# The inducing points' softmax in one pass over x with running maxima, on four column groups, with weights loaded later and layer 2 six chunks behind layer 1

## The chip, the cores and the metric

The kernel runs on one core of one Trainium2 chip. The metric is device time in microseconds of one execution; less is better. Three executions of the kernel before took 1043.28, 1042.4 and 1047.28 us, median 1043.28 us.

## The reference

`x` has 12480 tokens of 128 channels, `inducing` 32 points of 128 channels, and there are four weights of 128 by 2048 (or its transpose), handed over as float64.

```
h = softmax(inducing @ x.T / sqrt(128)) @ x          # 32 x 128
a = softmax(x @ h.T / sqrt(128)) @ h                 # 12480 x 128
g = a @ moe_w_in;   y1 = max(0.01 * g, g) @ moe_w_out
g = y1 @ moe2_w_in; g = where(g >= 1, g, where(g <= -1, 0, (g + 1)**2 / 4))
out = g @ moe2_w_out
```

## The kernel before

There are two phases. The **prologue** makes `HT`, that is h transposed (`HT` is written at L390). The **main phase** takes x again, transposed, in 26 chunks of 480 tokens, and each chunk through 16 slices of the hidden dimension: 416 steps `k` of layer 1, and 416 of layer 2, which follow `LAG` chunks and six steps later.

The order on every engine is the order in which the program is written (a manual schedule), so each engine works its own list strictly from the top; SyncE's list holds the DMAs.

**Prologue.** x comes in 13 pieces of 960 tokens (`load_x`), and 7 of the 26 chunks come a second time by channel (`xd`); after pieces 2, 4, 6 and 8 a quarter of a weight is loaded. `split_x(c)` transposes a chunk's four blocks on TensorE (L233), copies them out (`xT`, L235), and makes a high part (`xhi`) and a low part (`xlo`, mostly on GpSimd, L242) of the tokens for float32r products. `scores(c)` (L248) is one float32 product of 480 columns against a weight with the 32 points at one of four places and zeros beside them (`izf`), so that four chunks add up to a band of 128 rows. Two groups of bands have a maximum each (`maximum`), so the exponentials (`exps`, L283) start only when the maxima of a group are known; then `turn` (L293, L297, L298) transposes e back in two parts, and `gather` (L310, L311) multiplies it with `xhi` and `xlo`. `factors` and `denominator` bring the two groups together. Everything from the last scores to `HT` comes after x has landed.

**Weights.** `convert(n, q)` makes float32 of a quarter (512 columns) of a float64 weight: one operation on ScalarE (L103), four on VectorE (L104, L106, L108, L110), and then, for the first weight (n = 0), a sum on VectorE (L114), for the others a copy on ScalarE (L117) and two operations on GpSimd (L118, L119). There are 16 quarters (`units`). `work(n)` lists n of VectorE's operations, two quarters in turn; `ensure(n, j)` lists as many as slice j needs. In the program before, the prologue holds the conversions of 8 quarters (`CONV_1`, `WORK_1`, `WORK_2`): all of the first two weights.

**Start of the main phase.** `attend(0, ...)` makes chunk 0's softmax weights `aT`; `hidden(q, ...)` makes quarter q of `Gs` = h w_in (L419, L423, L426), from the first weight; step k multiplies `aT` with slice k of `Gs` (L549), takes `hi` (ScalarE, L552) and `lo` (VectorE, L559, or GpSimd, L557), and four steps later come three products with the second weight (L513 to L515). `linear` (steps 4 to 18) needs the second weight. After 16 slices a chunk of layer 1 ends with `x2hi` (ScalarE, L601) and `x2lo`. Layer 2 has six products of 480 columns a step, `cl`, `sq`, `g`, `hi`, `lo` on the other engines, and ends a chunk with `y` (L611). The conversions of the last 8 quarters stand one operation in every second step.

Of the kernel before, what the change touches and what calls it, by code (L numbers as in the profile page):

```python
# [9 lines left out]
F32 = mybir.dt.float32  # L10
# [60 lines left out]
def moe_kernel(ctx: ExitStack, tc, x_d, xt_d, it_d, w1_d, w2_d, w3_d, w4_d, y_d):  # L71
    """a = softmax(x h^T) with h from the inducing points; y = L4(act2(L3(L2(act1(L1(a h))))))
    with every operand of a large product as a sum of two float32r parts."""
# [5 lines left out]
    raw = ctx.enter_context(tc.tile_pool(name="raw", bufs=RAW))  # L79
    cv = ctx.enter_context(tc.tile_pool(name="cv", bufs=3))  # L80
# [5 lines left out]
    ahead = False       # whether a conversion's end makes place for the next load  # L86
# [42 lines left out]
    def work(n, until=len(units)):  # L129
        """n more operations of the conversions, two quarters in turn, up to a given number of them."""  # L130
# [33 lines left out]
    xe = inner.enter_context(tc.tile_pool(name="xe", bufs=1))  # L164
    xq = inner.enter_context(tc.tile_pool(name="xq", bufs=3))
    iz = inner.enter_context(tc.tile_pool(name="iz", bufs=1))

    xraw, xlo, xT = {}, {}, {}

    def load_x(i):  # L170
        for c in (2 * i, 2 * i + 1):
            if c in XT_DMA:
                t = xq.tile([C, CW], F32, name="xd", bufs=XD)
                nc.sync.dma_start(out=t, in_=xt_d[:, c * CW:(c + 1) * CW])
                xT[c] = t
# [42 lines left out]
    tb = (bank[6], bank[7])

    def rows(s):  # L220
        return min(SC, NCH - s * SC) * M

    def split_x(c):
        """A chunk by channel, and by token in two parts."""
        sl = slice(c * CB, (c + 1) * CB)
        i, h = divmod(c, 2)
        src = xraw[i][:, h * CB:(h + 1) * CB, :]
        if not h:       # the low part takes the place of the piece before
            xlo[i] = xs.tile([BT, 2 * CB, C], F32R, name="xlo", tag=f"x{i - 1}")
        if c not in XT_DMA:  # L230
            b = tb[c // 2 % 2]
            for q in range(CB):
                nc.tensor.transpose(b[:, q * BT:(q + 1) * BT], src[:, q, :], ident[:BT, :BT])  # L233
            t = xq.tile([C, CW], F32, name="xT")
            nc.scalar.activation(t, b[:, :CW], AF.Copy)  # L235
            xT[c] = t
        if c % XHI_DVE == XHI_DVE - 1:
            nc.vector.tensor_copy(out=xhi[:, sl, :], in_=src)
        else:
            nc.scalar.activation(xhi[:, sl, :], src, AF.Copy)  # L240
# [416 lines left out]
```

## Time and profile before

| | us |
|---|---|
| median of three executions | 1043.28 |
| span of the profiled execution (first to last instruction) | 1040.2 |
| median less span | 3.1 |
| `HT` ready | 78.0 |
| first chunk of layer 1 done (`x2hi` starts) | 105.8 |
| fourth chunk of layer 1 done | 154.5 |
| a chunk where both layers run | 36.3 |
| a chunk of layer 2 alone, at the end | 20.9 |

The profile's page is of one execution of 1040.2 us. It gives no time for what lies around the span; the median of the executions is 3.1 us above it. A row of the timeline gives the start, the length, the engine, the line and the tiles, and in brackets how long the engine had been idle and what ended that. A length for "x4" runs from the first start to the last end.

### The profile page before, as it was taken

Reading aid. Unit: us, or ns where it says so; the run is one execution under the profiler, and the core shown is the slowest. Engines: PE = TensorE matmul, PEld = TensorE weight load, DVE = VectorE, ACT = ScalarE, POOL = GpSimd, SP = SyncE. Lnnn points to the kernel's source line nnn. Section 1 sums busy time; section 2 is a strip of 40 time slices with the busy share of each in tenths; the row PEclk is TensorE's granted clock in tenths of the full one; section 3 lists DMA queues with packets and bytes.
Section 4 is the critical chain, followed back from the end, with each engine's and each line's share of the span. In section 5 each row is a group of like instructions: output and inputs, shape, how many; then the busy total and the mean of one; then the engine's idle time right before and its main releaser. Section 6 shows DMA issues by size and latency. Waiting matters only on the chain.

```text
span 1040.2 us, 15657 instructions
## 1 busy us (share of the span) xinstructions
PE 1018.7 (98%) x4956; PEld 862.0 (83%) x4956; DVE 835.2 (80%) x1491; ACT 835.1 (80%) x1605; POOL 686.0 (66%) x561
## 2 busy tenths in 40 slices
PE   8789999999999999999999999999999999999998
PEld 5377878888888888888888888888888888888887
DVE  4987998777787877778787777878877787878998
ACT  4537788888888888888888888888888888888997
POOL 5741647666666666666676666666666666667886
PEclk9989999999999999999999999999999999999999
DMA  9830300000000000000000000000000000000000
GB/s 242 242 92 10 109 12 10 20 1 20 20 1 20 20 20 1 20 20 1 20 20 20 1 20 19 6 15 20 20 1 20 20 10 1 10 10 10 11 10 20
DMA packets 12782, 30.30 MB, mean 29 GB/s; under 512 B 1539, under 2 KB 9091, under 8 KB 12699
## 3 DMA queue, kind: packets, MB, share of 16 engines
q1 hardware_dynamic: 12699, 29.30, 9.7%
q8 instruction: 39, 0.64, 0.3%
q14 instruction: 44, 0.36, 0.1%
HBM read 22.90 MB, written 6.39 MB: 28 GB/s over the span
## 4 chain that ended last, share of the span: by engine, by line
PE 89%; DVE 8%; DMA 2%; ACT 1%; issue 1%; SPq 0%; ACTq 0%; DVEq 0%
PE bank L513 25%; PE bank L515 25%; PE bank L514 25%; PE bank L549 8%; PE bank L471 2%; DVE lo L559 2%; DMA wraw<-in_w 1%; DVE cvb L110 1%; DVE cva L106 1%; DVE cvb L108 1%; PE bank L501 0%; DVE w L114 0%; PE bank L310 0%; PE bank L598 0%; DMA xraw<-in_x 0%
## 5 line engine op out<-in xcount | busy, mean ns | idle before, releaser
L575 POOL TENSOR_TENSOR lo<-g,hi 128x480 fp32r<-128x480 f32 x409 | 499.8, 1225 | 242.4 <-PE bank L514 162.1
L552 ACT ACTIVATE hi<-bank 128x480 fp32r<-128x480 f32 x416 | 236.1, 573 | 132.2 <-PE bank L549 129.7
L515 PE MATMUL bank<-lo,whi 128*128 128x480 f32 x832 | 316.4, 380 | 0.0
L513 PE MATMUL bank<-hi,whi 128*128 128x480 f32 x832 | 316.4, 380 | 0.0
L514 PE MATMUL bank<-hi,wlo 128*128 128x480 f32 x832 | 315.7, 379 | 0.0
L586 DVE SCALAR_TENSOR_TENSOR g<-bank,sq 128x480 f32<-128x480 f32 x416 | 270.0, 649 | 38.9 <-ACT sq L563 38.9
L563 ACT ACTIVATE sq<-cl,half 128x480 f32<-128x480 f32 x416 | 289.2, 695 | 9.6 <-DVE cl L582 5.2
L559 DVE SCALAR_TENSOR_TENSOR lo<-bank,hi 128x480 fp32r<-128x480 f32 x316 | 205.5, 654 | 110.5 <-ACT hi L552 110.2
L582 DVE TENSOR_SCALAR cl<-bank 128x480 f32<-128x480 f32 x416 | 270.4, 650 | 19.7 <-PE bank L515 13.7
L570 ACT ACTIVATE hi<-g 128x480 fp32r<-128x480 f32 x416 | 249.1, 599 | 0.5 <-DVE g L586 0.5
L515 PEld LDWEIGHTS bank<-lo,whi 128*128 128x128 f32 x832 | 156.0, 188 | 26.7 <-POOL lo L557 0.9
L514 PEld LDWEIGHTS bank<-hi,wlo 128*128 128x128 f32 x832 | 156.7, 188 | 25.0
L513 PEld LDWEIGHTS bank<-hi,whi 128*128 128x128 f32 x832 | 156.3, 188 | 24.8 <-ACT y L611 0.4
L557 POOL TENSOR_TENSOR lo<-r,hi 128x480 fp32r<-128x480 f32 x100 | 125.3, 1253 | 60.9 <-ACT r L556 57.5
L549 PE MATMUL bank<-aT,Gs 96*128 96x480 f32 x416 | 162.8, 393 | 0.0
L513 PE MATMUL bank<-x2hi,whi 128*128 128x480 f32 x416 | 159.1, 383 | 0.6 <-DVE g L586 0.6
L515 PE MATMUL bank<-x2lo,whi 128*128 128x480 f32 x416 | 157.9, 380 | 0.0
L514 PE MATMUL bank<-x2hi,wlo 128*128 128x480 f32 x416 | 157.8, 379 | 0.0
L514 PEld LDWEIGHTS bank<-x2hi,wlo 128*128 128x128 f32 x416 | 78.9, 190 | 12.6
L513 PEld LDWEIGHTS bank<-x2hi,whi 128*128 128x128 f32 x416 | 78.8, 190 | 12.6 <-DVE g L586 1.3
L515 PEld LDWEIGHTS bank<-x2lo,whi 128*128 128x128 f32 x416 | 78.1, 188 | 12.7
L549 PEld LDWEIGHTS bank<-aT,Gs 96*128 96x128 f32 x416 | 78.2, 188 | 12.1 <-DVE lo L559 0.4
(115 smaller groups left out, 666.6 us busy)
## 6 DMA issues: line engine op xcount, KB each, us to landing
wraw<-in_w SPq DMA_DIRECT2D x16, 512.0 KB, 4.7
xraw<-in_x SPq DMA_DIRECT2D x13, 480.0 KB, 13.2
xt<-in_xt SPq DMA_DIRECT2D x26, 240.0 KB, 2.7
out_y<-y SPq DMA_DIRECT2D x26, 240.0 KB, 2.0
xd<-in_xt SPq DMA_DIRECT2D x7, 240.0 KB, 13.3
iT<-in_it SPq DMA_DIRECT2D x1, 16.0 KB, 1.9
```

Source lines behind the costliest of these rows:

```text
L513: nc.tensor.matmul(out, lhsT=whi[n][:, sl], rhs=hi, start=start, stop=False)
L514: nc.tensor.matmul(out, lhsT=wlo[n][:, sl], rhs=hi, start=False, stop=False)
L515: nc.tensor.matmul(out, lhsT=whi[n][:, sl], rhs=lo, start=False, stop=stop)
L549: nc.tensor.matmul(p1, lhsT=Gs[:, j * 128:(j + 1) * 128], rhs=aT[c], start=True, stop=True)
L552: nc.scalar.activation(hi, p1, AF.Relu)
L557: nc.gpsimd.tensor_tensor(out=lo, in0=r, in1=hi.bitcast(F32), op=ALU.subtract)
L559: nc.vector.scalar_tensor_tensor(out=lo, in0=p1, scalar=0.0, in1=hi.bitcast(F32), op0=ALU.max, op1=ALU.subtract)
L563: nc.scalar.activation(sq, cls.pop(kb - 1), AF.Square, scale=-0.5, bias=half)
L570: nc.scalar.activation(hi, g, AF.Copy)
L575: nc.gpsimd.tensor_tensor(out=lo, in0=g, in1=hi.bitcast(F32), op=ALU.subtract)
L582: nc.vector.tensor_scalar(out=cl, in0=p3, scalar1=1.0, scalar2=-1.0, op0=ALU.min, op1=ALU.max)
L586: nc.vector.scalar_tensor_tensor(out=g, in0=b3[(kb - 1) % 3][:, :CW], scalar=-1.0, in1=sqs.pop(kb - 1), op0=ALU.max, op1=ALU.add)
```

## The change

- x comes by token in ten bands: the 12480 tokens are four groups of 3120, and a band is `BANDS[s]` tokens of each group. The last two bands come a second time by channel (`xl`), the other `xd` loads are gone, and so are `xhi` and `xlo`.
- `scores(s)` is four float32 products, one for each group, with a weight of 32 columns, into four places of 32 rows of one bank. Each band has its own maximum, the least bias so far (`nm`), its exponentials at once, and a factor `alpha`. `gather(s)` is four float32 products of 32 weight columns for each block of 128 tokens, likewise into four places; `add_up` keeps the running sums `R` and `D`. It follows one band behind.
- Two quarters of weights are loaded between the bands, four more behind x. Two quarters are converted in the prologue (`UNTIL_S`) in place of eight; the first weight's sum goes to GpSimd; `units` is reordered.
- `hidden(2)` and `hidden(3)` stand after steps 1 and 3, with the conversions that they need.
- `LAG` is 6 in place of 4; `warm` is gone.

```diff
-RAW = 4
-LAG = 4
+RAW = 6
+LAG = 6
+G4 = 4
+BANDS = (48, 128, 256, 512, 512, 512, 512, 384, 128, 128)
+XL = 2
+XT_DVE = 4
+LOAD_W = (3, 4)
+WORK_S = ((0, 0), (0, 0), (0, 0), (0, 0), (1, 2), (2, 3), (2, 3), (2, 2), (0, 1), (0, 0))
+UNTIL_S = (0, 0, 0, 0, 1, 2, 2, 2, 2, 2)
+HIDDEN = (1, 3)
...
-            yield
-            nc.vector.tensor_tensor(out=w1[:, sl], in0=a, in1=b, op=ALU.add)
+            nc.gpsimd.tensor_tensor(out=w1[:, sl], in0=a, in1=b, op=ALU.add)
...
-    units = [(n, q) for n in range(4) for q in range(NQ)]
+    units = [(0, 0), (0, 1), (0, 2), (1, 0), (0, 3), (1, 1), (1, 2), (1, 3)] + [(n, q) for n in (2, 3) for q in range(NQ)]
...
+    for s, w in enumerate(BANDS):
+        p, nb = min(w, 128), -(-w // 128)
+        if s == NS_B - XL:
+            xl = xs.tile([C, XL, G4, 128], F32, name="xl")
+            nc.sync.dma_start(out=xl.rearrange("p s q t -> p (s q t)"), in_=xl_d)
...
+        nc.sync.dma_start(out=t.rearrange("p q b c -> p (q b c)"), in_=src)
+        xb[s] = t
+        if s in LOAD_W:
+            load_next_w()
+    load_xt(0)
+    for _ in range(RAW - len(LOAD_W)):
+        load_next_w()
...
+    def by_channel(s):
...
+        for g in range(0, len(flat), 4):
...
+            for i, (q, b) in enumerate(part):
+                nc.tensor.transpose(ps_t[:, i * p:(i + 1) * p], xb[s][:, q, b, :], ident[:p, :p])
+            dst, src = t[:, g * p:(g + len(part)) * p], ps_t[:, :len(part) * p]
+            if k % XT_DVE == 1:
+                nc.vector.tensor_copy(out=dst, in_=src)
+            else:
+                nc.scalar.activation(dst, src, AF.Copy)
+    def scores(s):
+        p = b_S[s % 2]
+        for q in range(G4):
+            nc.tensor.matmul(p[q * M:(q + 1) * M, :w], lhsT=iT, rhs=xT[s][:, q * w:(q + 1) * w], start=True, stop=True)
+        nc.vector.tensor_reduce(out=mx[:, s:s + 1], in_=p[:, :w], op=ALU.max, axis=AX.X)
...
+            nc.vector.scalar_tensor_tensor(out=nm[:, s:s + 1], in0=mx[:, s:s + 1], scalar=-SCALE, in1=nm[:, s - 1:s],
+                                           op0=ALU.mult, op1=ALU.min)
+        nc.scalar.activation(e[:, :w], p[:, :w], AF.Exp, scale=SCALE, bias=nm[:, s:s + 1], accum_out=ssum[:, s:s + 1])
+        if s:
+            nc.scalar.activation(alpha[:, s:s + 1], nm[:, s - 1:s], AF.Exp, scale=-1.0, bias=nm[:, s:s + 1])
+    def turn(s):
+        for b in range(nb):
+            nc.tensor.transpose(b_U[:p, b * 128:(b + 1) * 128], es[s][:, b * p:(b + 1) * p], ident)
+        nc.scalar.activation(t[:p, :nb * 128], b_U[:p, :nb * 128], AF.Copy)
+    def gather(s):
+        for b in range(nb):
+            for q in range(G4):
+                nc.tensor.matmul(A[q * M:(q + 1) * M], lhsT=eTs[s][:p, b * 128 + q * M:b * 128 + (q + 1) * M],
+                                 rhs=xb[s][:, q, b, :], start=(b == 0), stop=(b == nb - 1))
...
+    for s in range(NS_B):
+        if s not in xT:
+            by_channel(s)
+        if s:
+            turn(s - 1)
+        scores(s)
+        work(WORK_S[s][0], UNTIL_S[s])
+        if s:
+            gather(s - 1)
+            add_up(s - 1)
+        work(WORK_S[s][1], UNTIL_S[s])
...
+        if k in HIDDEN:
+            q = 2 + HIDDEN.index(k)
+            ensure(0, 4 * q)
+            for p in range(3):
+                hidden(q, p)
```

**What moved, on TensorE, in the prologue.** Before, around chunks 1 to 4 (four transposes of x, then one product of 480 columns into a bank of 128 rows):

```order
L233 MATMUL bank_85<-ident,xraw 128x120 x4
L248 MATMUL bank_78<-xT,izf 128x480
L233 MATMUL bank_85<-ident,xraw 128x120 x4
L248 MATMUL bank_78<-xd,izf 128x480
L233 MATMUL bank_84<-ident,xraw 128x120 x4
L248 MATMUL bank_78<-xT,izf 128x480 x2
```

and in the change, around one band of 512 (`e` is the band before's exponentials, `eT` those turned):

```order
L227 MATMUL bank_83<-ident,xb 128x128 x4
L227 MATMUL bank_81<-ident,xb 128x128 x4
L227 MATMUL bank_82<-ident,xb 128x128 x4
L227 MATMUL bank_83<-ident,xb 128x128 x4
L257 MATMUL bank_86<-ident,e 128x128 x4
L239 MATMUL bank_84<-xT,iT 32x512 x4
L268 MATMUL bank_87<-xb,eT 32x128 x16
```

The products with e, which stood in one block behind all scores, stand between the bands, and both kinds write 32 rows at a time.

**On VectorE, at the start of the main phase.** Before (`s` is the last of `attend(0)`, `Gs` are `hidden`, the `lo` are steps 0, 1, 2 and so on):

```order
L495 TENSOR_TENSOR s<-ea,s 120x4x32
L426 SCALAR_TENSOR_TENSOR Gs<-bank_80,Gs 32x512
L426 SCALAR_TENSOR_TENSOR Gs<-bank_79,Gs 32x512
L426 SCALAR_TENSOR_TENSOR Gs<-bank_85,Gs 32x512
L559 SCALAR_TENSOR_TENSOR lo_893<-bank_81,hi_892 128x480
L426 SCALAR_TENSOR_TENSOR Gs<-bank_80,Gs 32x512
L559 SCALAR_TENSOR_TENSOR lo_900<-bank_82,hi_899 128x480
L559 SCALAR_TENSOR_TENSOR lo_905<-bank_83,hi_904 128x480
L559 SCALAR_TENSOR_TENSOR lo_910<-bank_84,hi_909 128x480
```

and in the change, from step 0's `lo`:

```order
L484 SCALAR_TENSOR_TENSOR lo_666<-bank_84,hi_665 128x480
L484 SCALAR_TENSOR_TENSOR lo_671<-bank_85,hi_670 128x480
L100 TENSOR_SCALAR cvb<-wraw 128x512 x2
L102 SCALAR_TENSOR_TENSOR cva<-cva,cvb 128x512 x2
L104 TENSOR_SCALAR cvb<-cva 128x512 x2
L106 SCALAR_TENSOR_TENSOR cvb<-wraw,cvb 128x512
L351 SCALAR_TENSOR_TENSOR Gs<-bank_82,Gs 32x512
L484 SCALAR_TENSOR_TENSOR lo_695<-bank_86,hi_694 128x480
L484 SCALAR_TENSOR_TENSOR lo_700<-bank_87,hi_699 128x480
L106 SCALAR_TENSOR_TENSOR cvb<-wraw,cvb 128x512
L100 TENSOR_SCALAR cvb<-wraw 128x512 x2
L102 SCALAR_TENSOR_TENSOR cva<-cva,cvb 128x512 x2
```

Fifteen operations of conversions (seven, then eight) now stand between step 1 and step 4, where there were none.

**On TensorE, the same place.** Before:

```order
L471 MATMUL bank_78<-HT,xt 120x32 x4
L419 MATMUL bank_80<-w_88,HT 96x512
L419 MATMUL bank_79<-w_88,HT 96x512
L419 MATMUL bank_85<-w_88,HT 96x512
L501 MATMUL bank_78<-identr,s 96x120 x4
L419 MATMUL bank_80<-w_88,HT 96x512
L549 MATMUL bank_81<-aT,Gs 128x480
```

and in the change:

```order
L396 MATMUL bank_81<-HT,xt 120x32 x4
L344 MATMUL bank_83<-w_91,HT 96x512
L344 MATMUL bank_82<-w_91,HT 96x512
L426 MATMUL bank_81<-identr,s 96x120 x4
L474 MATMUL bank_84<-aT,Gs 128x480
L474 MATMUL bank_85<-aT,Gs 128x480
L344 MATMUL bank_82<-w_91,HT 96x512
L474 MATMUL bank_86<-aT,Gs 128x480
L474 MATMUL bank_87<-aT,Gs 128x480
L344 MATMUL bank_83<-w_91,HT 96x512
L474 MATMUL bank_88<-aT,Gs 128x480
```

The third and fourth `hidden` product stand behind steps 1 and 3, and the steps behind them wait in TensorE's list.

## Rows read from the trace of the kernel before

**Rows 1.** The page: span, busy time by engine, the chain by engine.

```profile
span 1040.2 us, 15657 instructions
PE 1018.7 (98%) x4956; PEld 862.0 (83%) x4956; DVE 835.2 (80%) x1491; ACT 835.1 (80%) x1605; POOL 686.0 (66%) x561
...
PE 89%; DVE 8%; DMA 2%; ACT 1%; issue 1%; SPq 0%; ACTq 0%; DVEq 0%
```

**Rows 2.** Windows by stage: busy PE, PEld, DVE, ACT, POOL; PEclk, DMA share, GB/s.

```profile
20.00:49.00 29.00, 23.24 (x96) 11.68 (x97) 28.29 (x35) 19.62 (x40) 20.88 (x14) 1.00 0.95 253
49.00:78.00 29.00, 22.57 (x243) 20.78 (x241) 24.18 (x43) 9.37 (x23) 15.00 (x10) 0.82 0.33 103
...
106.00:155.00 49.00, 47.94 (x233) 39.45 (x232) 47.36 (x87) 40.27 (x86) 29.17 (x22) 1.00 0.20 64
```

**Rows 3.** Timeline of VectorE at the end of the prologue.

```profile
73.30 1.05 DVE L346 TENSOR_SCALAR ssum<-ssum,f 128x3 f32<-128x3 f32 x2
...
77.72 0.26 DVE L390 TENSOR_TENSOR HT<-bank,rden 128x96 f32<-128x96 f32 x1 [1.00 <-PE bank L388]
```

**Rows 4.** Timeline of ScalarE: ends of chunks, layer 1 (L601) and layer 2 (L611).

```profile
105.83 0.57 ACT L601 ACTIVATE x2hi<-bank 128x480 fp32r<-128x480 f32 x1
...
154.53 0.58 ACT L601 ACTIVATE x2hi<-bank 128x480 fp32r<-128x480 f32 x1
...
222.56 0.57 ACT L601 ACTIVATE x2hi<-bank 128x480 fp32r<-128x480 f32 x1
...
258.82 0.57 ACT L601 ACTIVATE x2hi<-bank 128x480 fp32r<-128x480 f32 x1
...
997.85 0.57 ACT L611 ACTIVATE y<-bank 128x480 f32<-128x480 f32 x1
...
1018.74 0.57 ACT L611 ACTIVATE y<-bank 128x480 f32<-128x480 f32 x1
```

**Rows 5.** Timeline of VectorE: the first two weight quarters land.

```profile
13.13 0.43 DVE L104 TENSOR_SCALAR cvb<-wraw 128x512 uint32<-128x512 uint32 x1 [4.11 <-DMA wraw<-in_w]
...
19.74 0.43 DVE L104 TENSOR_SCALAR cvb<-wraw 128x512 uint32<-128x512 uint32 x1 [3.29 <-DMA wraw<-in_w]
```

**Rows 6.** Timeline of TensorE: transposes and scores, early and at full clock.

```profile
11.88 1.82 PE L248 MATMUL bank<-xd,izf 128*128 128x480 f32 x2
...
24.88 0.63 PE L233 MATMUL bank<-ident,xraw 120*128 120x120 f32 x4 [0.23 <-DMA xraw<-in_x]
25.35 1.78 PE L248 MATMUL bank<-xT,izf 128*128 128x480 f32 x4
...
28.96 0.98 PE L248 MATMUL bank<-xT,izf 128*128 128x480 f32 x2
```

**Rows 7.** Timeline of TensorE: products with e right behind transposes.

```profile
66.84 0.30 PE L310 MATMUL bank<-xhi,eT 120*64 120x128 f32 x1
66.98 0.22 PE L311 MATMUL bank<-xlo,eT 120*64 120x128 f32 x1
67.04 0.23 PE L310 MATMUL bank<-xhi,eT 120*64 120x128 f32 x1
```

**Rows 8.** Timeline of ScalarE: step 0 of the main phase.

```profile
83.95 0.57 ACT L552 ACTIVATE hi<-bank 128x480 fp32r<-128x480 f32 x1 [0.83 <-PE bank L549]
```

**Rows 9.** Timeline of VectorE: conversions alone, and one beside GpSimd.

```profile
65.08 0.68 DVE L110 SCALAR_TENSOR_TENSOR cvb<-wraw,cvb 128x512 f32<-128x512 uint32 x1
65.68 0.41 DVE L108 TENSOR_SCALAR cvb<-cva 128x512 uint32<-128x512 uint32 x1
...
92.71 1.45 DVE L104 TENSOR_SCALAR cvb<-wraw 128x512 uint32<-128x512 uint32 x1
```

**Rows 10.** Groups by line and form: GpSimd's sum of a quarter.

```profile
L119 POOL TENSOR_TENSOR wlo<-cva,cvb 128x512 fp32r<-128x512 f32 x12 | 16.0, 1335 | 3.4 <-DVE cvb L110 2.8
```

**Rows 11.** Windows: TensorE's clock falls after a wait, and rises.

```profile
54.00:55.00 1.00, 0.26 (x2) 0.26 (x3) 0.66 (x2) 0.00 (x0) 0.00 (x0) 0.80 0.00 0
...
61.00:62.00 1.00, 1.00 (x14) 1.00 (x13) 1.00 (x2) 0.24 (x1) 0.32 (x1) 0.79 0.69 184
```

More of the change, by code (lines that the diff above doesn't have):

```diff
@@ L218, in moe_kernel @@
[L218 to L238, printed above, removed]
-        else:
-            nc.scalar.activation(xhi[:, sl, :], src, AF.Copy)
-        eng = nc.vector if c % XLO_DVE == XLO_DVE - 1 else nc.gpsimd
-        eng.tensor_tensor(out=xlo[i][:, h * CB:(h + 1) * CB, :], in0=src, in1=xhi[:, sl, :].bitcast(F32), op=ALU.subtract)
@@ L244, in scores @@
-    def scores(c):
-        s, q = divmod(c, SC)
-        p = score[s][:, :CW]
-        last = q == SC - 1 or c == NCH - 1
-        nc.tensor.matmul(p, lhsT=izf[:, q].rearrange("p r m -> p (r m)"), rhs=xT.pop(c), start=(q == 0), stop=last)
-        if last:
-            r = rows(s)
-            if r < 128:
-                nc.vector.tensor_copy(out=smax[:, s:s + 1], in_=smax[:, s - 1:s])
-            nc.vector.tensor_reduce(out=smax[:r, s:s + 1], in_=p[:r], op=ALU.max, axis=AX.X)
-    nmax = const.tile([128, 2], F32, name="nmax")
@@ L285, in exps @@
         es[s] = e
     def turn(s):
-        r = rows(s)
-        e = es[s]
-        b = tb[s % 2]
-        for q in range(CB):
-            nc.tensor.transpose(b[:BT, q * 128:q * 128 + r], e[:r, q * BT:(q + 1) * BT], ident[:r, :r])
-        t = xe.tile([BT, CB, SC, 2, M], F32R, name="eT", bufs=2)
-        src = b[:BT, :].rearrange("p (b c m) -> p b c m", c=SC, m=M)[:, :, :r // M, :]
-        hi, lo = t[:, :, :r // M, 0, :], t[:, :, :r // M, 1, :]
-        nc.scalar.activation(hi, src, AF.Copy)
@@ L298, in turn @@
-        nc.vector.tensor_tensor(out=lo, in0=src, in1=hi.bitcast(F32), op=ALU.subtract)
-        es[s] = t
-    def gather(s, half):
-        t = es[s]
-        g = int(s >= NSA)
-        for q in range(2 * half, 2 * half + 2):
-            for c in range(rows(s) // M):
-                i = (s * SC + c) * CB + q
-                lhsT = t[:, q, c].rearrange("p r m -> p (r m)")
-                first = s in (0, NSA) and q == 0 and c == 0
-                last = s in (NSA - 1, NSB - 1) and q == CB - 1 and c == rows(s) // M - 1
-                nc.tensor.matmul(bH[g][:2 * M, :C], lhsT=lhsT, rhs=xhi[:, i, :], start=first, stop=False)
-                nc.tensor.matmul(bH[g][:2 * M, :C], lhsT=lhsT, rhs=xlo[i // (2 * CB)][:, i % (2 * CB), :], start=False, stop=last)
@@ L313, in moe_kernel @@
-    g0, g1 = maximum(0), maximum(1)
-    for c in range(NCH):
-        split_x(c)
-        if c >= AHEAD:
-            scores(c - AHEAD)
-        if c >= CONV_FROM:
-            work(WORK_1[c % len(WORK_1)], CONV_1)
-        if c - NSA * SC in (1 + AHEAD, 2 + AHEAD, 3 + AHEAD):
-            next(g0)
-        if c in EXP_A:
-            exps(EXP_A.index(c))
-        if c in TURN_A:
-            turn(TURN_A.index(c))
-    for c in range(NCH - AHEAD, NCH - 1):
-        scores(c)
-    scores(NCH - 1)
@@ L358, in follow @@
-    def follow(h):
-        if h in MAX_B:
-            next(g1)
-        for r, k in enumerate(EXP_B):
-            if k == h:
-                exps(NSA + r)
-    d = denominator()
-    next(g1)
-    for s in range(NSB):
-        if len(TURN_A) <= s + 1 < NSB:
-            turn(s + 1)
-        if s == 2:
-            factors()
-        if s == NSB - 2:
-            next(d)
-        gather(s, 0)
-        follow(2 * s)
-        if s == NSB - 1:
-            rden = next(d)
-            nc.scalar.activation(hrow[0], bH[0][:2 * M, :C], AF.Copy)
-        gather(s, 1)
-        follow(2 * s + 1)
-        if s < NSB - 2:
-            work(WORK_2, 2 * NQ)
@@ new lines, in moe_kernel @@
+    denb = const.tile([128, C], F32, name="denb")
+    for s in range(NS_B):
[9 more added lines that the diff above has]
+        work(WORK_S[s][1], UNTIL_S[s])
+    last = nm[:, NS_B - 1:NS_B]
+    nc.tensor.transpose(b_M[:1, :128], last, ident)
+    mrow = small.tile([1, G4, M], F32, name="mrow")
+    nc.vector.tensor_reduce(out=mrow[:, 0, :], in_=b_M[:1, :128].rearrange("p (q m) -> p m q", m=M), op=ALU.min, axis=AX.X)
@@ new lines, in moe_kernel @@
+    nc.vector.tensor_copy(out=mrow[:, 1:, :], in_=mrow[:, :1, :].to_broadcast([1, G4 - 1, M]))
+    turn(NS_B - 1)
+    nc.tensor.matmul(b_M[:, 128:129], lhsT=mrow.rearrange("p q m -> p (q m)"), rhs=ones[:1, :1], start=True, stop=True)
+    top = small.tile([128, 1], F32, name="top")
+    nc.vector.tensor_copy(out=top, in_=b_M[:, 128:129])
+    f = small.tile([128, 1], F32, name="f")
+    nc.scalar.activation(f, last, AF.Exp, scale=-1.0, bias=top)
+    fsel = const.tile([128, M], F32, name="fsel")
@@ new lines, in moe_kernel @@
+    nc.vector.tensor_scalar(out=fsel, in0=sel, scalar1=f, scalar2=None, op0=ALU.mult)
+    gather(NS_B - 1)
+    add_up(NS_B - 1)
+    nc.tensor.matmul(b_M[:, 256:256 + M], lhsT=denb, rhs=fsel, start=True, stop=True)
+    nc.tensor.matmul(b_M[:, 384:384 + M], lhsT=R, rhs=fsel, start=True, stop=True)
+    rden = small.tile([C, M], F32, name="rden")
+    nc.vector.tensor_scalar(out=rden, in0=b_M[:, 256:256 + M], scalar1=EPS, scalar2=None, op0=ALU.add)
+    nc.vector.reciprocal(out=rden, in_=rden)
@@ L517, in moe_kernel @@
     attend(0, 0)
-    for q in range(3):
+    for q in (0, 1):
+        ensure(0, 4 * q)
         hidden(q, 0)
-    for part in (1, 2, 3):
-        attend(0, part)
+    attend(0, 1)
     hidden(0, 1)
+    attend(0, 2)
+    hidden(0, 2)
+    attend(0, 3)
     attend(0, 4)
-    hidden(0, 2)
     attend(0, 5)
     hidden(1, 1)
-    hidden(2, 1)
     attend(0, 6)
     hidden(1, 2)
-    hidden(2, 2)
-    hidden(3, 0)
     NS = NCH * NJ
@@ L543, in moe_kernel @@
         if kb == 0:
+            work(4 * len(units))
             fill.close()
```

189 lines of the change are left out of this document (76 added, 113 removed).

## The prediction, made before the change was run

> **What bounds the kernel now.** I read the page first. TensorE is busy for 98% of a span of 1040.2 us and is 89% of the chain that ended last [rows 1], so time is to be had only where TensorE waits. The windows by stage say where that is. From 20 to 49 us the DMA engines are at 0.95 and VectorE at 28.29 of 29 us; from 49 to 78 us x has landed, and yet `HT` is 29 us away: no engine is full, and the granted clock is 0.82 [rows 2]. The last operation of the prologue is `HT`, at 77.98 [rows 3]. From 106 to 155 us, layer 1 alone, VectorE is the full one (47.36 of 49) [rows 2].
>
> The ends of chunks price the main phase [rows 4]. Chunk 0 of layer 1 ends 27.9 us behind `HT` (105.83 - 77.98). The next three take 48.7 us, 16.2 each. With both layers a chunk takes 36.3 (258.82 - 222.56), and layer 2 alone 20.9. Layer 1 would thus cost TensorE 15.4 (36.3 - 20.9), and the conversions hold it up by 0.9 a chunk.
>
> **The prologue: a new price, with two ends.** First the DMA. The first two quarters of weights land at 13.13 and 19.74 us [rows 5]; by the queue's order 1.75 MB lie between them, so 0.265 MB/us, and with the 2.51 MB ahead of the first, landing = 3.7 us + bytes at that rate. The changed order has 1.95 MB up to the first band of 512, which lands at 11, and 7.99 MB up to the last x: 33.8 us. (Before, x ends near 49, because 1.7 MB of `xd` and two more quarters lie between.)
>
> Then TensorE, from the first band of 512 on. Four transposes take 0.47 us (24.88 to 25.35). A float32 product stands as two records; one takes 0.98 and two take 1.78, so another costs 0.80 per 480 columns, 1.67 ns a column [rows 6]. The bands left need 76 transposes of x and 22 of e, 98 x 0.118 = 11.5 us; scores of 2688 columns four times over, 10752 x 1.67 ns = 17.9 us; and 88 products of 128 columns with e, 18.8 us. One behind the other this is 48.2 us. If the four groups run side by side, the products shrink to a quarter, and the sum is 20.7 us.
>
> No two products of the trace go to different column groups, so nothing shows which it is. I take a value between. The two records of a product use the same 32 columns, so the second must follow the first; if the engine starts records in their order, the first record of group 1 can run beside the second of group 0, but not before it. Of the eight passes of four products five stay visible: scores 11.2 us, and of the 32 passes of sixteen products 17: 10.0 us. Sum 32.7 us. A change between full-width and narrow products: behind transposes the next product comes 0.14 us later and then every 0.06 [rows 7], so 0.08; two in each of seven bands make 1.1 us.
>
> The Trainium skill (TensorEngine Tiling (Array Packing), Key Properties) says that changing the tiling mode, not just the tile, drains TensorE. By that rule each change would cost what a product takes beyond its spacing, 0.18 us, and the sum would be 2.5 us in place of 1.1; the row says 0.08 for 128 to 64 columns, and no row shows 32.
>
> The small bands ahead hold TensorE until about 12.0 (half-clock products take 1.82 in place of 0.98 there [rows 6]). Behind the last product come `D`, `denb`, `R`, two products, the reciprocal and `HT`, as before from 73.30 to 77.98 [rows 3]: 4.7 us, and 0.3 for the maximum's way over the groups, which lies partly beside `gather`. So `HT` at 12.0 + 32.7 + 1.1 + 5.0 = **50.8 us**, 27.2 earlier. Ends: 12.0 + 48.2 + 2.5 + 5.3 = 68; and with full overlap the DMA binds, 33.8 + the last bands + 5 = about 43 to 46. ScalarE and VectorE lose `xhi`, `xlo` and six conversions there and cost nothing: some 24 us of VectorE's work lie beside 33 of TensorE.
>
> **The start of the main phase: a loss.** Before, step 0's `hi` starts 6.0 us behind `HT` [rows 8]. Now ScalarE's copy of the first quarter of `Gs` stands ahead of `attend`'s exponential, and VectorE's part of it ahead of the sums: +1.0, so 7.0. Two `lo` follow, to 8.7. Then VectorE has seven operations of conversions: the starts 65.08, 65.68, 66.02 [rows 9] give 0.60 and 0.34, so 3.2 us, to 11.9; GpSimd adds 1.34 [rows 10], to 13.2. Only now can the third `hidden` product run, and step 2 stands behind it in TensorE's list. TensorE has waited 6 us. After waits shorter than that its clock fell to half at 54 us and rose only past 61 [rows 11], so I count the 512 columns at half: 1.9 us, to 15.1. Copy, low part and two `lo`: 17.6. Eight more operations, 3.8 us alone, but GpSimd's two subtractions for the second weight run beside them, and a conversion beside GpSimd takes 1.45 in place of 0.41 [rows 9]; with two such 5.9, to 23.5; GpSimd 24.8; product 26.7. From here chunk 0 goes as before from step 0, 21.9 us (83.95 to 105.83), less what runs already: **48.4 us behind `HT` in place of 27.9, +20.5**. Ends: every conversion alone and full clock, 44; all of them beside GpSimd and half clock for longer, 52. Who waits there: layer 1's steps 2 and 4, and with them everything.
>
> The weights' DMAs cost nothing: the four quarters behind x land by 43, before they are wanted; SP waits for raw buffers only with loads that are needed later.
>
> **LAG.** Two chunks of both layers become two of layer 1 and two of layer 2: -72.5 + 41.8 + (30.7 to 32.5, without or with conversions beside them), 0 to +1.7. All conversions now end before layer 2 starts; I take +0.7.
>
> **Sum.** -27.2 + 20.5 + 0.7 = -6.0: span 1034.2, and with the 3.1 us by which the median stands above the span, **1037.3 us**.
>
> **Rivals.**
> 1. *All four groups run side by side.* For it: the four places are disjoint, and nothing in the program makes one wait for another. Against: the order of the records. `HT` at about 45, -33 + 20.5 + 0.7 = -11.8: 1031.5. Chance 0.28. The Trainium skill (TensorE: Matmul & The Clock Gate, Part 3) reports 2.38 times for three narrow products at once; that is nearer to this rival than to mine.
> 2. *No overlap, the prologue bound by TensorE; slower.* The place is bands 3 to 9: 9.2 us of TensorE for a band of 512 against 4 us of DMA, `HT` at 68. For it: no row shows two products at a time, and L248 pairs stand strictly 0.80 apart. Against: they use all 128 columns. -10 + 20.5 + 0.7 = +11.2: 1054.5. It decides once `HT` comes later than 56.8 (78.0 - 21.2). Chance 0.17.
> 3. *The start costs more.* Partial overlap as in mine, but conversions contend with GpSimd throughout and the clock stays at half across both waits: +28 in place of +20.5, 1045. For it: VectorE is the full engine from 106 to 155 with the same operations. Against: GpSimd has far less to do there than in the prologue before. Chance 0.10.
>
> **How the numbers follow.** My forecast has 0.45. Its own range, by `HT` from 46 to 55 and chunk 0 from 44 to 51, is 1028 to 1044. A measurement tells about 0.5%, 5.2 us, so the bounds are 1038.1 and 1048.5. Of the 0.45 some 0.26 lie below, 0.18 within, 0.01 above; of rival 1 0.26 and 0.02; rival 2 0.02 within and 0.15 above; rival 3 0.01, 0.05, 0.04. Together faster 0.53, same 0.27, slower 0.20. The range goes from rival 1 with a start that costs only 16 (1025) to rival 2 (1054.5).
>
> **What would show it.** Right: `HT` near 51; in the trace, narrow float32 products that start about half a product apart, 0.43 us for 512 columns; VectorE with seven and eight conversions between steps 1 and 4, TensorE idle for 6 and then 6 to 8 us before the third and fourth `hidden` product, at a granted clock of 0.5; the first `x2hi` some 48 us behind `HT`; chunks of both layers still 36.3. Wrong: narrow products 0.85 us apart (rival 2), or four in 0.9 us and TensorE waiting for x (rival 1); a third `hidden` product that waits for nothing; chunks of layer 2 alone that take more than 20.9, which would make the longer lag cost.

## The result, and the profile after

The changed kernel takes 1057.88 us (median of four executions, 1057.74 to 1061.1) against 1043.16 of the kernel before in the same job: ratio 1.0148, 95% interval 1.0123 to 1.0173. It is slower by 15 us, where 6 us less were forecast, and above the end of the range. The profiled execution has a span of 1055.8 us, 15.6 above that of before. The page:

```profile
span 1055.8 us, 15700 instructions
...
PE 1007.7 (95%) x4980; PEld 852.8 (81%) x4980; DVE 817.7 (77%) x1494; ACT 830.7 (79%) x1599; POOL 655.4 (62%) x539
...
PE 89%; DVE 4%; POOL 3%; ACT 2%; issue 2%; ACTq 0%; POOLq 0%; DVEq 0%
```

TensorE's work has become 11 us less (1018.7 in [rows 1]), and its share has fallen from 98% to 95%: it waits more than it has saved. GpSimd, absent from the chain before, has 3% of it. Where that is, the timelines of VectorE and ScalarE show, at the places of [rows 3, 4]:

```profile
45.49 0.26 DVE L316 TENSOR_TENSOR HT<-bank,rden 128x96 f32<-128x96 f32 x1
```

```profile
107.39 0.58 ACT L526 ACTIVATE x2hi<-bank 128x480 fp32r<-128x480 f32 x1
...
202.23 0.58 ACT L526 ACTIVATE x2hi<-bank 128x480 fp32r<-128x480 f32 x1
...
249.88 0.57 ACT L536 ACTIVATE y<-bank 128x480 f32<-128x480 f32 x1 [0.33 <-PE bank L440]
286.13 0.57 ACT L536 ACTIVATE y<-bank 128x480 f32<-128x480 f32 x1 [0.31 <-PE bank L440]
...
971.68 0.57 ACT L536 ACTIVATE y<-bank 128x480 f32<-128x480 f32 x1
992.59 0.57 ACT L536 ACTIVATE y<-bank 128x480 f32<-128x480 f32 x1
```

| | before | after | difference | forecast |
|---|---|---|---|---|
| `HT` ready | 77.98 | 45.75 | -32.2 | -27.2 |
| from there to the first `x2hi` | 27.85 | 61.64 | +33.8 | +20.5 |
| the rest | 934.4 | 948.4 | +14.0 | +0.7 |
| span | 1040.2 | 1055.8 | +15.6 | -6.0 |

Chunks of both layers still take 36.25 us and chunks of layer 2 alone 20.9, so the third difference lies in the chunks of layer 1 alone: from the first `x2hi` to the sixth 94.84 us, 19.0 a chunk, where three took 16.2 each before [rows 4]. The windows of the changed kernel (columns as in [rows 2]):

```profile
14.00:20.00 6.00, 5.38 (x58) 3.53 (x56) 1.93 (x5) 3.63 (x9) 0.00 (x0) 1.00 1.01 420
20.00:32.00 12.00, 9.87 (x125) 7.21 (x117) 8.83 (x18) 7.17 (x16) 2.39 (x2) 1.00 0.90 343
32.00:46.00 14.00, 10.55 (x162) 6.86 (x154) 7.40 (x28) 5.90 (x19) 0.28 (x1) 0.97 0.17 56
46.00:55.00 9.00, 6.83 (x18) 3.58 (x18) 3.17 (x9) 2.37 (x7) 0.00 (x0) 0.50 0.00 0
55.00:75.00 20.00, 5.17 (x8) 1.99 (x8) 11.91 (x20) 5.24 (x10) 5.10 (x4) 0.50 0.29 85
75.00:107.40 32.40, 24.95 (x130) 19.35 (x129) 18.70 (x33) 18.15 (x39) 11.97 (x9) 0.83 0.20 60
...
126.00:145.00 19.00, 16.31 (x78) 13.28 (x77) 15.29 (x29) 13.88 (x29) 9.98 (x7) 0.98 0.05 14
```

Up to 46 us TensorE has the highest share of the five engines and VectorE has room; TensorE waits for no load of x from 12 us on, though the DMA engines are full up to 20 us and at 0.90 up to 32. From 46 to 75 us TensorE's clock is at its lower level, 0.50, and in the twenty microseconds from 55 on it does 5 us of work. The waits that end there, and behind it, in TensorE's timeline:

```profile
47.42 3.71 PE L344 MATMUL bank<-w,HT 128*96 128x512 f32 x4
...
61.34 2.02 PE L344 MATMUL bank<-w,HT 128*96 128x512 f32 x2 [6.00 <-POOL w L109]
...
72.99 2.02 PE L344 MATMUL bank<-w,HT 128*96 128x512 f32 x2 [8.83 <-POOL w L109]
...
84.06 0.48 PE L439 MATMUL bank<-hi,wlo 128*128 128x480 f32 x1 [2.01 <-POOL wlo L114]
...
91.98 0.49 PE L438 MATMUL bank<-hi,whi 128*128 128x480 f32 x1 [1.70 <-ACT whi L112]
...
96.15 0.77 PE L439 MATMUL bank<-hi,wlo 128*128 128x480 f32 x1 [3.68 <-POOL wlo L114]
```

The first two were forecast (6 us, then 6 to 8). The last three were not: they stand at slices 4 and 8 of chunk 0, the first that need the second and the third quarter of the second weight, so these quarters are late as well. In chunks 1 to 4 one wait stands in each, and GpSimd's timeline says why:

```profile
117.24 0.38 PE L474 MATMUL bank<-aT,Gs 96*128 96x480 f32 x1
...
124.47 0.48 PE L440 MATMUL bank<-lo,whi 128*128 128x480 f32 x1 [2.22 <-POOL lo L482]
```

```profile
116.71 1.86 POOL L113 TENSOR_TENSOR cva<-cva,whi 128x512 f32<-128x512 f32 x1 [1.55 <-ACT whi L112]
118.65 1.63 POOL L114 TENSOR_TENSOR wlo<-cva,cvb 128x512 fp32r<-128x512 f32 x1
120.23 1.48 POOL L113 TENSOR_TENSOR cva<-cva,whi 128x512 f32<-128x512 f32 x1
121.79 1.28 POOL L114 TENSOR_TENSOR wlo<-cva,cvb 128x512 fp32r<-128x512 f32 x1
123.03 1.39 POOL L482 TENSOR_TENSOR lo<-r,hi 128x480 fp32r<-128x480 f32 x1
```

`work` takes two running conversions in turn, a piece each, so both end in neighbouring calls, and their four operations on GpSimd, 6.3 us, stand together. Behind them stands the low part of slice 14 (the third of GpSimd's slices in the chunk; the expectations of e1 and e2 take it for slice 9, whose low part was done before the pile, at 113.94). TensorE wants it four steps after its product, here at 122.25, 5.0 us behind the product's start at 117.24. In the kernel before two conversions end close together as well, but a slice's low part stood between the two and another behind them, so that no slice stood behind more than one conversion:

```profile
121.05 1.29 POOL L118 TENSOR_TENSOR cva<-cva,whi 128x512 f32<-128x512 f32 x1 [1.21 <-ACT whi L117]
123.04 1.28 POOL L119 TENSOR_TENSOR wlo<-cva,cvb 128x512 fp32r<-128x512 f32 x1 [0.70 <-DVE cvb L110]
124.27 1.69 POOL L557 TENSOR_TENSOR lo<-r,hi 128x480 fp32r<-128x480 f32 x1
125.92 1.28 POOL L118 TENSOR_TENSOR cva<-cva,whi 128x512 f32<-128x512 f32 x1
127.28 1.36 POOL L119 TENSOR_TENSOR wlo<-cva,cvb 128x512 fp32r<-128x512 f32 x1
129.03 1.21 POOL L557 TENSOR_TENSOR lo<-r,hi 128x480 fp32r<-128x480 f32 x1 [0.39 <-ACT r L556]
```

### The profile page after: what moved, and what is told of

Same layout as the page of the kernel before. It is cut to its first block, busy times and chain, and to the rows that moved or that the text cites. A ratio compares the mean times of both kernels' runs of the same rounds, so it can differ in the third digit from the quotient of the medians.

```text
span 1055.8 us, 15700 instructions
## 1 busy us (share of the span) xinstructions
PE 1007.7 (95%) x4980; PEld 852.8 (81%) x4980; DVE 817.7 (77%) x1494; ACT 830.7 (79%) x1599; POOL 655.4 (62%) x539
## 4 chain that ended last, share of the span: by engine, by line
PE 89%; DVE 4%; POOL 3%; ACT 2%; issue 2%; ACTq 0%; POOLq 0%; DVEq 0%
PE bank L440 25%; PE bank L439 25%; PE bank L438 25%; PE bank L474 8%; PE bank L396 2%; POOL cva L113 1%; DVE lo L484 1%; PE bank L239 1%; PE bank L426 1%; PE bank L523 1%; POOL lo L482 1%; PE bank L344 1%; POOL wlo L114 1%; ACT hi L477 1%; DVE cvb L106 0%
## 5 line engine op out<-in xcount | busy, mean ns | idle before, releaser
L482 POOL TENSOR_TENSOR lo<-r,hi 128x480 fp32r<-128x480 f32 x98 | 120.9, 1234 | 92.4 <-ACT r L481 70.9
L474 PE MATMUL bank<-aT,Gs 96*128 96x480 f32 x416 | 167.7, 404 | 2.4 <-ACT aT L433 1.7
## 6 DMA issues: line engine op xcount, KB each, us to landing
xl<-in_xl SPq DMA_DIRECT2D x1, 512.0 KB, 16.2
```

The costliest lines, as they stand in the source:

```text
L474: nc.tensor.matmul(p1, lhsT=Gs[:, j * 128:(j + 1) * 128], rhs=aT[c], start=True, stop=True)
L482: nc.gpsimd.tensor_tensor(out=lo, in0=r, in1=hi.bitcast(F32), op=ALU.subtract)
```

## The experiments

Two theories came out of that. **A**: the start is dear because its conversions are not done when `HT` comes. **B**: chunks 1 to 4 are dear because the conversions pile up on GpSimd ahead of a slice. The rivals: **C**, the longer lag costs by itself; and that the sum of the conversions' work is the bound, wherever it stands. In the table, "start" is from `HT` to the first `x2hi`, "chunks 1 to 5" from there to the sixth; ratios are to the kernel before.

| run | `HT` | start | chunks 1 to 5 | span | median | ratio, interval |
|---|---|---|---|---|---|---|
| the change | 45.75 | 61.6 | 94.8 | 1055.8 | 1057.88 | 1.0148, 1.0123 to 1.0173 |
| e1 lag 5 | 45.96 | 61.2 | 79.7 (four) | 1057.6 | 1060.07 | 1.0161, 1.0124 to 1.0198 |
| e2 slices moved | 47.34 | 61.2 | 88.0 | 1050.1 | 1051.01 | 1.0074, 1.005 to 1.0099 |
| e3 six in the prologue | 55.90 | 43.9 | 96.4 | 1049.8 | 1052.08 | 1.0078, 1.0047 to 1.0109 |
| e4 products turned | 48.46 | 63.0 | 94.8 | 1059.8 | 1061.96 | one execution |
| e6 conversions apart | 47.39 | 64.6 | 83.3 | 1048.9 | 1046.68 | 1.0042, 1.0025 to 1.0059 |
| e8 four, early | 49.75 | 52.1 | 96.3 | 1051.7 | 1053.83 | 1.0102, 1.0077 to 1.0127 |
| e7 together | 50.86 | 49.0 | 82.2 | 1035.5 | 1037.6 | 0.9953, 0.9936 to 0.997 |
| e9 four steps ahead | 51.84 | 42.9 | 84.8 | 1033.2 | 1032.11 | 0.989, 0.9866 to 0.9914 |
| e10 more slices | 48.90 | 44.0 | 83.9 | 1030.4 | 1032.11 | 0.9897, 0.9879 to 0.9916 |
| e11 as e9, lag 5 | 51.74 | 43.2 | 68.7 (four) | 1033.5 | 1034.46 | 0.9907, 0.9887 to 0.9928 |

The prologue is the same in the change, e1, e2 and e6, and `HT` comes between 45.75 and 47.39; it is the same in e9, e10 and e11, and comes between 48.90 and 51.84. So differences of up to 3 us in `HT` mean nothing here.

**e1: the lag.**

```diff
-LAG = 6
+LAG = 5
```

> The changed kernel with layer 2 five chunks behind layer 1 in place of six, nothing else. Theory B (in chunks 1 to 4 TensorE waits 2.2 us a chunk for GpSimd, whose two conversions stand together ahead of slice 9; the lag itself is cheap): the chunk that goes is the last one without conversions, 17.1 us, so 17.1 + 20.9 - 36.2 = 1.8 us less, about 1056; the four waits stay. Rival C (the longer lag is what costs 14 us, through its chunks of one layer): 7 us less for one chunk of two, about 1051.

The span grew by 1.8 us, so C falls: one chunk less of lag should have given 7 back. The 1.8 us less that B gave were missed too. The four waits stayed, one line of the table of waits (chunks 1 to 4):

```profile
PE bank L440 <- POOL lo L482: 8.4, 4, 2.2
```

but those four chunks took 79.7 us in place of 77.7, at a granted clock of 0.93 from 108 us on (1.00 up to 127 in the change), and the first chunk of both layers 49.8 in place of 47.7, with conversions just ahead of it.

**e2: GpSimd's slices moved.**

```diff
-POOL_LO1_FILL = (3, 9, 14)
+POOL_LO1_FILL = (3, 12, 15)
```

> The changed kernel with GpSimd's slices of layer 1 in chunks 1 to 5 at steps 3, 12 and 15 in place of 3, 9 and 14, so that the second of them stands behind the two conversions, by the order of steps. Theory B: the four waits of 2.2 us on that low part go, and with them the fall of the clock behind each; chunks 1 to 5 take 16.3 to 17 us in place of 19, 10 to 13 us less: 1045 to 1048. Rival (the conversions' operations on VectorE and ScalarE are the bound of these chunks, and GpSimd's wait only shows it): the wait moves to another operation, chunks still 18.5 to 19, within 2 us of 1058.

6.8 us less in these chunks, short of the 10 to 13 that B gave. The long wait went, and two short ones came, on slices 12 and 15, each of which now stands behind one of the two conversions:

```profile
140.14 0.48 PE L440 MATMUL bank<-lo,whi 128*128 128x480 f32 x1 [0.69 <-POOL lo L482]
...
144.18 0.48 PE L440 MATMUL bank<-lo,whi 128*128 128x480 f32 x1 [1.14 <-POOL lo L482]
```

The clock stayed at 1.00 all through. This could not tell B from the rival of the summed work; e6 could.

**e6: conversions apart.** As much work, but one conversion at a time.

```diff
+        if k == 14:
+            most[0] = 1
...
-        while len(running) < 2 and ...
+        while len(running) < most[0] and ...
```

> The changed kernel with one conversion running at a time from step 14 of chunk 0 on, in place of two in step with each other: GpSimd's two operations of a conversion come every eight steps, not four of them together every sixteen; as much work as before. Theory B (it is the pile of four operations ahead of a slice): chunks 1 to 4 take 16.4 to 17 us in place of 18.7 to 20.2, as in the kernel before, 9 to 13 us less: 1045 to 1049. Rival (the conversions' work is what these chunks are bound by, and moving the slices alone has given all that there is): chunks 18 us or more, no better than the run with the slices moved, 1051.

Chunks 1 to 4 take 17.0 us each (128.99 to 145.94), at the end of B's range and below the rival's 18, and the waits on GpSimd have shrunk from 8.5 us to 2.2:

```profile
128.99 0.58 ACT L528 ACTIVATE x2hi<-bank 128x480 fp32r<-128x480 f32 x1
145.94 0.58 ACT L528 ACTIVATE x2hi<-bank 128x480 fp32r<-128x480 f32 x1
```

```profile
PE bank L440 <- POOL lo L484: 2.2, 4, 0.6
```

So B is shown: with the same work in the same chunks, its spacing alone is worth 11.6 us of the 14.0. The waits themselves are 6.3 of the 11.6; beside the rest stands a granted clock of 1.00 from 108 to 202 us, where the change has 1.00 up to 127, then 0.98, and from 145 us on 0.90 to 0.93. The median fell by 11.2. The start was 3.0 us longer in the profiled execution, which is 4 us above the median of its ten; one conversion at a time also holds at the end of chunk 0.

**e3: six conversions in the prologue.**

```diff
-WORK_S = (..., (1, 2), (2, 3), (2, 3), (2, 2), (0, 1), (0, 0))
-UNTIL_S = (0, 0, 0, 0, 1, 2, 2, 2, 2, 2)
+WORK_S = (..., (1, 2), (2, 3), (2, 3), (3, 3), (3, 2), (0, 0))
+UNTIL_S = (0, 0, 0, 0, 1, 2, 4, 6, 6, 6)
```

> The changed kernel with six conversions in the prologue in place of two (four more, of which two for the second weight, from the band at 32 us on, where VectorE has gaps). Theory A (the start of the main phase is dear because its conversions are not done): HT comes 0 to 5 us later than 45.8, the waits of 6.0 and 8.8 us before the third and fourth hidden product go, no half clock from 54 to 75, the first x2hi stands 30 to 38 us behind HT in place of 61.6: 18 to 30 us less, 1028 to 1040. Rival (VectorE's sum of work up to the first x2hi is the bound, and four conversions cost in the prologue what they cost in chunk 0): HT 12 us or more later, in all within 8 us of 1058. Chunks 1 to 4 stay at 18.7 to 20 by both.

Between the two: the start fell by 17.8 us, but `HT` came 10.2 later. Both waits on the first weight are gone, and 1.7 and 4.2 us on the second remain. VectorE, busy 9.93 of 10 us from 40 to 50, does conversions beside GpSimd in the small last bands, where the chain of maximum, exponential and products has nothing else to hide them:

```profile
42.33 2.72 DVE L100 TENSOR_SCALAR cvb<-wraw 128x512 uint32<-128x512 uint32 x2
...
55.64 0.26 DVE L316 TENSOR_TENSOR HT<-bank,rden 128x96 f32<-128x96 f32 x1
```

These two operations take 0.76 us together where GpSimd is idle. A is right on where the start's time goes, and wrong in that it can be had for nothing. The clock that A expected did not come back either: it is granted at 0.50 from 44 to 64 us.

**e8: four conversions, early.**

```diff
-LOAD_W = (3, 4)
-WORK_S = (..., (0, 0), (1, 2), (2, 3), (2, 3), (2, 2), (0, 1), (0, 0))
-UNTIL_S = (0, 0, 0, 0, 1, 2, 2, 2, 2, 2)
+LOAD_W = (3, 4, 5, 6)
+WORK_S = (..., (0, 2), (2, 2), (2, 3), (2, 3), (0, 0), (0, 0), (0, 0))
+UNTIL_S = (0, 0, 0, 2, 3, 4, 4, 4, 4, 4)
```

> The changed kernel with four conversions in the prologue in place of two, all in the bands from 14 to 36 us, none in the small last bands, and two more quarters of weights loaded between the bands of x. Theory A (a conversion done in VectorE's gaps of the prologue is free, one in the small last bands or in chunk 0 is paid in full): HT 0 to 3 us later than 45.8, the wait of 6.0 us before the third hidden product gone, the one of 8.8 before the fourth still there, first x2hi 50 to 55 us behind HT in place of 61.6: 4 to 10 us less, 1048 to 1054. Rival (every conversion in the prologue delays HT by its VectorE time of 2.2 us or more, as the four more conversions delayed it by 10): HT 5 us or more later, within 4 us of 1058.

4.1 us less: start 9.5 less, `HT` 4.0 later, little more than its scatter. One of the waits on the first weight is left (6.3 us). Part of what it cost is ScalarE's first piece of the conversions, two of them ahead of the copies of `xT` that TensorE waits for: 1.7 us in place of 0.6 behind the first pair below, and 2.2 in place of 0.8 behind the next, whose second piece waits 0.75 us for GpSimd as well:

```profile
18.21 1.19 ACT L99 ACTIVATE cva<-wraw 128x512 f32<-128x512 f32 x2
19.32 1.06 ACT L232 ACTIVATE xT<-bank 128x512 f32<-128x512 f32 x2
...
30.60 0.67 ACT L99 ACTIVATE cva<-wraw 128x512 f32<-128x512 f32 x1 [0.75 <-POOL w L109]
```

**e7: together.** e8's prologue, one conversion at a time from step 0 on, and in chunk 0 a piece in each step:

```diff
-HIDDEN = (1, 3)
+HIDDEN = (1, 7)
...
-POOL_LO1_0 = (4, 8, 12)
+POOL_LO1_0 = (2, 6, 10)
...
+        if k == 0:
+            most[0] = 1
...
-        work(WORK[k % len(WORK)] if k >= WORK_FROM else 0)
+        work(1 if k < NJ else WORK[k % len(WORK)])
```

> All together: four conversions in the prologue as in the run above, from chunk 0 on one conversion at a time and in chunk 0 one of its pieces in each step from step 0 on, so that each quarter is done by the step that needs it; the fourth hidden product behind step 7 in place of 3; chunk 0's slices for GpSimd at 2, 6 and 10. Theories A and B: HT 0 to 3 us later than 45.8, no wait over 3 us in chunk 0 and its first x2hi 32 to 40 us behind HT in place of 61.6, chunks 1 to 5 16.4 to 17 us: 28 to 40 us less, 1018 to 1030, faster than both kernels. Rival (VectorE's sum of work binds the stretch from 20 to 200 us): 45 us or more behind HT or chunks of 18 us, 1038 or more.

20 us less than the change, and 0.5% faster than the kernel before, but short of the forecast: the start is 49.0, not 32 to 40, which is where the rival had it (45 or more), while chunks 1 to 4 take 16.4 to 16.8 as by B. Each of the second weight's last three quarters was done just after the step that wants it:

```profile
PE bank L439 <- POOL wlo L114: 7.8, 3, 2.8
```

**e9: four steps ahead.** The pieces of one quarter stand in VectorE's gaps between `HT` and step 0:

```diff
+    most[0] = 1
+    work(1)
     attend(0, 1)
     hidden(0, 1)
+    work(1)
     attend(0, 2)
...
     hidden(1, 2)
+    work(2)
```

`HIDDEN` is that of the change again, `POOL_LO1_0` stays at (2, 6, 10), and the prologue's conversions start one band later.

> The run with everything together, mended in three places: in the prologue no conversion's piece before 20 us (one at 17 us held ScalarE up for 2.2 us, as its weight had not landed); the third quarter of conversions' pieces stand in the gaps of VectorE between HT and step 0 (1.8, 1.8 and 1.4 us long), so that chunk 0's conversions run four steps ahead; the fourth hidden product back at step 3. Theory A: HT 2 us earlier than 50.6, the three waits on the second weight (2.2, 2.8, 2.8 us) and the one on the fourth hidden product's bank (2.7) gone, first x2hi 38 to 42 us behind HT in place of 49.3: 8 to 13 us less than 1037.6, 1025 to 1030. Rival (VectorE's work binds, so what is moved ahead comes back as another wait): 45 us or more behind HT, 1033 or more.

Start 42.9, 6.1 less, and 5.5 us less in the median: the three waits on the second weight are gone. The numbers lie between A's (38 to 42, 1025 to 1030) and the rival's (45 or more, 1033 or more). Three things of the expectation failed. `HT` was not earlier. The piece put down to a late weight had not waited for one, as the rows of e8 above show: ScalarE has no idle time before the pair at 18.21, and the longer hold-up, of 2.2 us, lies behind the pair at 30.60. And a new wait stands at the end of chunk 0, on VectorE, which is busy 18.16 of 20 us from 75 to 95:

```profile
PE bank L527 <- DVE Qs L386: 3.0, 1, 3.0
PE bank L366 <- DVE Gs L351: 1.8, 1, 1.8
```

**e10: more slices for GpSimd in chunk 0.**

```diff
-POOL_LO1_0 = (4, 8, 12)
+POOL_LO1_0 = (2, 6, 9, 10, 13, 14)
```

> The run with the conversions four steps ahead, with six slices of chunk 0 on GpSimd (2, 6, 9, 10, 13, 14) in place of three (4, 8, 12). If VectorE's work is what chunk 0 is bound by in the end (18.2 of 20 us busy from 75 to 95, and 3.0 us of TensorE's wait on it before the last product): VectorE has 2 us less to do, the wait of 3.0 us goes: 2 to 4 us less, 1028 to 1030. Rival (GpSimd's operations make VectorE's longer, and its slices queue behind conversions): no gain or a loss, 1032 to 1036, with TensorE waiting for a slice or for the second weight.

The rest is as in e9, whose slices on GpSimd are 2, 6 and 10, not 4, 8 and 12 as the expectation has it. No gain (1032.11 both times; start 44.0 for 42.9), as the rival had it. The wait that was to go has not:

```profile
PE bank L527 <- DVE Qs L386: 3.5, 1, 3.5
```

Three low parts fewer on VectorE are given back there; that its other operations grow longer beside GpSimd's is likely, but was not taken apart.

**e11: the lag, without the pile.** `LAG = 5` on e9.

> The run with the conversions four steps ahead, with layer 2 five chunks behind layer 1 in place of six. By the finding that the lag is cheap where no conversion stands in TensorE's way: a chunk of layer 1 alone of 15.6 us (179.61 - 164.03) and one of layer 2 alone of 20.9 are given for one of both of 36.2, 0.3 us less: 1032, within 1 us. Rival (the longer lag costs, 7 us a chunk): 1025. Rival (the sixth chunk is needed, since conversions reach into it): 1034 or more.

The spans are 1033.5 and 1033.2. The median is 2.3 us above that of e9, where the second rival had it (1034 or more), but the intervals overlap, so the run does not tell that rival from the theory. The 7 us of the first rival did not come: where no conversion stands in TensorE's way, a chunk of lag costs nothing that can be measured.

**e4: the products' order.**

```diff
-        for b in range(nb):
-            for q in range(G4):
+        for q in range(G4):
+            for b in range(nb):
```

> The changed kernel with the loops of the products with e turned round: a group's blocks one behind the other, then the next group, so that neighbours go to the same column group. Theory (narrow products of different groups run side by side): sixteen products of a band of 512 take 16 x 0.21 = 3.4 us in place of 1.3, five such bands and the small ones some 11 us more of TensorE, HT 6 to 11 us later than 45.8. Rival (a narrow product is simply short, wherever it stands): 1.3 us again, HT within 1 us.

First the change: four scores of 512 columns from 18.97 to 19.85, and sixteen products of 128 columns from 19.85 to 21.14; then the turned order.

```profile
18.97 1.37 PE L239 MATMUL bank<-xT,iT 128*32 128x512 f32 x8
19.85 1.36 PE L268 MATMUL bank<-xb,eT 128*32 128x128 f32 x32
21.14 1.53 PE L227 MATMUL bank<-ident,xb 128*128 128x128 f32 x12
```

```profile
20.13 2.44 PE L268 MATMUL bank<-xb,eT 128*32 128x128 f32 x32
22.50 2.06 PE L227 MATMUL bank<-ident,xb 128*128 128x128 f32 x16
```

1.29 us become 2.37 by the order alone, so neighbours in different column groups do run side by side. But 2.37 is below the 3.4 of the price in [rows 6]; why, stays open. `HT` came 2.7 later, within its scatter, not 6 to 11; TensorE then waits 1.0 us for the copies of `xT` in place of 2.6, so that part of the loss was hidden.

## Why the prediction was wrong

**The prologue: right direction, wrong pick, and the error in its favour.** "I take a value between", with five of eight passes visible, was wrong; rival 1 holds. Four scores of 512 columns take 0.88 us where one takes 0.85 by [rows 6] (0.80 for 480). `HT` at 45.75 lies in rival 1's "about 45", but that is in part luck. Rival 1 had x as the bound, and TensorE does not wait for x. A band of 512 takes TensorE 5.5 us (18.44 to 23.91), where the forecast's own prices with full overlap give 4.1; the sixteen products with e take 1.29 of it in place of 0.86, and the rest is mainly the transposes, with the wait for the copies of `xT` in them. The argument that failed is "if the engine starts records in their order, the first record of group 1 can run beside the second of group 0, but not before it": the trace shows no such order holding the groups up. For the scores the gain is 3.9 times; the Trainium skill (TensorE: Matmul & The Clock Gate, Part 3) has 2.38 for three narrow products, a smaller share of what is possible than the 3.9 of four here. The change between kinds of product took 0.06 us (four transposes from 18.44, 0.47 us, the first score at 18.97): that price did not matter, and the drain that the Trainium skill states (TensorEngine Tiling (Array Packing), Key Properties) does not show as more.

**The start: the mechanism was right, and its end was missed.** The waits of 6.00 and 8.83 us and the half clock are what the prediction's working of the start describes. The fourth `hidden` product starts 27.2 us behind `HT`, forecast 24.8; the 2.4 go with the clock, which is already at half when `HT` comes (0.50 from 46 us on, and 3.71 us for the two first `hidden` products). In the kernel before it was 1.00 from 76 us on, and three such products took 2.79:

```profile
76.44 0.68 PE L201 MATMUL bank<-whi 128*128 128x512 f32 x2
...
77.61 0.73 PE L201 MATMUL bank<-whi 128*128 128x512 f32 x2
...
78.94 2.79 PE L419 MATMUL bank<-w,HT 128*96 128x512 f32 x6
```

The products of L201 are `warm`: their results are not used, they only fill TensorE's time ahead of `HT`. The change leaves them out, and the prediction put that at nothing. In the kernel with the change TensorE waits 0.9 and 1.0 us there. No run put them back, so what they are worth is not shown.

The step that failed is "from here chunk 0 goes as before from step 0, 21.9 us". Before, all eight quarters of the first two weights had been converted in the prologue. Now the second weight's four quarters were made in chunk 0, among and behind the last two of the first on VectorE and GpSimd, and TensorE waited 2.0 us for the second and 1.7 and 3.7 us for the third. That is 7.4 of the other 10.9 us; the granted clock of 0.83 from 75 to 107 us stands beside the rest. The runs bear it out: with four more conversions in the prologue the start is 43.9, and with them ahead of their steps 42.9, in place of 61.6. What is left against the 27.9 of the kernel before was not taken apart; in e9, too, the granted clock is 0.50 from 46 to 64 us.

**The lag: the step that failed is "I take +0.7".** It measured +14.0. "30.7 to 32.5, without or with conversions beside them" took the price of a chunk with conversions from before. There a slice lay between two conversions' operations on GpSimd; by the order of the program, the new order of `units` and the conversions' places in chunk 0 moved their ends against the slices by some steps (no run takes these two apart). The prediction did not follow the conversions past chunk 0. e6 gives back 11.6 of the 14.0 by spacing alone; e1 and e11 show that it is not the lag.

**The rivals.** Rival 1 was right on the overlap and had the same start, so it missed too. Rival 3 had the right place (a start of +28, measured +33.8). None followed the conversions to the second weight's later quarters or into chunks 1 to 4, where GpSimd holds the slices up.

In all: -5.0 (prologue) + 13.3 (start) + 13.3 (the rest) = 21.6, the distance from the forecast's span of 1034.2 to 1055.8. e9 keeps the change's bands, column groups and lag, mends both losses in part, and is 1.1% faster than the kernel before.

## What to carry to other kernels

Work taken off a prologue is only a gain if it is followed to where it is done instead, to its last piece: write down for each piece the step that wants it, and count what stands ahead of it on every engine on its way. Two background jobs that are served in turn end together, and their pieces on a shared engine pile up; how that falls against the foreground's pieces can change with an edit ahead of it. The same work one job at a time was worth 11 us here. An experiment that only moves a victim of such a pile shows less than one that takes the pile apart.

## What the runs showed of the hardware

Narrow float32 products in four column groups overlap almost fully at 512 columns (0.22 us each) and well at 128 (0.08 each; 0.15 when neighbours go to the same group). x came in faster than in the kernel before, at as full a DMA share, 420 GB/s against the 268 of this row of before:

```profile
14.00:20.00 6.00, 5.66 (x24) 2.65 (x22) 2.57 (x4) 3.02 (x6) 3.39 (x3) 1.00 1.01 268
```

A partition's row of a band has 8 KB in place of 4 KB, which may be why; no run tried it. And one wait of 2.2 us in a chunk, four times, went with a granted clock of 0.93 in those chunks in e1, and of 1.00, 0.98, 0.93 and 0.92 one after the other in the change, where two waits of 0.7 and 1.1 us a chunk left it at 1.00 (e2).
